# Fourier layer and soft mixture of experts on one core: the chains of batches 5 and 6 take the spacing of batches 0 to 4, and a product's scaling moves from VectorE to ScalarE and GpSimd

## The chip, the cores and the metric

The kernel runs on one core of a Trainium2 chip. The metric is device time in microseconds (us) of one launch. A core has five engines with a queue of instructions each: TensorE (PE in the rows; PEld is its weight load), VectorE (DVE), ScalarE (ACT), GpSimd (POOL) and SyncE (SP). Each executes its own instructions strictly in order, and waits on semaphores for the others. Nearly all DMAs are issued by SP's queue, also in order.

## The reference, cut to what matters

```python
X = rfft(x, axis=1)                         # x: 8 batches, 2496 rows, 256 columns
Yr = Xr @ w_r - Xi @ w_i + b_r
Yi = Xr @ w_i + Xi @ w_r + b_i
Y  = shrink(Yr, 0.01) + 1j * shrink(Yi, 0.01)
y  = irfft(Y, n=2496, axis=1)               # then all 8 * 2496 rows together:
logits = y @ phi                            # 32 slots, 4 for each of 8 experts
d  = softmax of logits over all rows
slot_input = d.T @ y
slot_out = for each expert: relu(slot_input[e] @ w1[e]) @ w2[e]
out = softmax(logits, over the 32 slots) @ slot_out
```

## The kernel before

**Transforms as products.** The length 2496 is 39 times 64. A first stage (products `pa`, results `ast`, written to DRAM as `adr`) transforms along 39. A second (`px`, read back as `ap`) transforms along 64. A batch then has five groups of four frequencies, and a group is one *step*: 40 steps in all, numbered s = 5 * batch + group. In a step PE computes `px` (two halves), `pk` and `py` (the linear layer), DVE and GpSimd form `rt` (the shrunk spectrum), and PE computes `pq` (the spectrum times phi, giving `p_sb`) and the transposes `pt`, whose copies `T` are kept until the batch's slots can be summed. To keep precision, fast products are made three times, from a value split into a rounded part (`xh`, `ch...`) and the rest (`xl`, `cl...`); the rounding is a copy, the rest a subtraction.

**The chain of a batch.** When its five steps are done, a batch b runs a chain beside the steps of the following batches (`c_stages`): the small spectrum `p_sb` is transformed back by `pg`, written to DRAM (`gd`), read back in another layout (`gp`), transformed by `pL` into logits `L`; `mx`, `pm`, `mall`, `pb` find and spread a running maximum; `ee` is the exponential; `pe` (to `ea`, DRAM `ed`, back as `eb`) and `pd` transform the exponentials forward; `dd` is `pd` times a constant, and the five products `pr` sum the slots out of `T` with `dd`. Batch 7, the last, has a chain of its own (`last_chain`), after which come the experts (`hps`, `po`) and the output.

**What sets the order.** Each piece of work is a generator that yields the time at which its next part is to be recorded, and a heap records them in that order; one unit of these times is a quarter of a step, a batch is 20 units. The times are hints for the order alone: they come from the table `PLAN`. In `c_stages` t0 is 20b + 26, and `pg`, `pL`, `pm`, `pb`, `pe`, `pd`, `pr` are offsets from it. `PLAN["late"]` replaces them for batches 4, 5 and 6. Before, batches 5 and 6 were packed closer than 0 to 4. TB (166) is the time at which the last step's own work ends.

**Places of tiles.** A tile is taken from one of a few pools under a tag with a fixed number of buffers, taken in turn; who takes one waits until its former content has been read. The transposes `pt` of batch 6 waited until after TB (`tp_t`, `late`), and its `rt` lay in buffers of the tag "T". `ps` is one bank of PSUM, used by `pg`, `pL`, `pm`, `pb`, `pe` and `pd` in turn.

**The product pd.** `halves` makes a product in two halves: it splits both sources (ACT rounds, `E_("cl_")`, DVE, subtracts), and for each half records the product and calls `evac`. For `pd` this was one DVE instruction that reads PSUM, multiplies by `dsc` and writes `dd`.

Of the kernel before, what the change touches and what calls it, by code (L numbers as in the profile page):

```python
# [23 lines left out]
S = 32  # L24
# [5 lines left out]
KG = 4  # L30
# [20 lines left out]
def _constants():  # L51
# [73 lines left out]
    "c0": 0.05,  # L125
    "pg": [1.35, 2.3],
    "pL": [6.6, 7.3],
    "pm": 8.35,
    "pb": 9.45,
    "pe": [11.35, 12.35],  # L130
    "cm": 14.3,
    "pd": [16.75, 17.5],
    "pr": [20.49, 24.49, 28.49, 32.489999999999995, 36.489999999999995],
    "au": [1.4, 18.85, 19.7],
    "tho": 1.4,
# [6 lines left out]
    "ko": 0.915,  # L142
    "to": 0.7,
    "ws": [-29, -28.9, -28.8, 2],
    "late": {'6': {'cms': [19.75, 19.71, 860.75, 862, 864, 865], 'pd': [20.36, 20.37], 'pr': [31.55, 31.6, 31.65, 31.7, 31.75], 'pL': [5.4, 5.8], 'pm': 6.875, 'pb': 7.325, 'pe': [8.75, 9.75], 'pg': [0.875, 1.275], 'fr': {'sinv': 0, 'm2': 0, 'f1': 0, 'suni': 0}}, '5': {'pg': [1.1, 1.8], 'pL': [4.95, 5.75], 'pm': 6.8, 'pb': 7.15, 'pe': [9.2, 9.9], 'pd': [13.8, 14.8], 'pr': [15.0, 17.25, 19.5, 21.75, 24.0]}, '4': {'pr': [18.4, 20.49, 24.49, 28.49, 32.49]}},
    "T_": {'wl': [[-45, 'r'], [-44, 'r'], [-43, 'r'], [-31.0, 't'], [-30.7, 't'], [-29.4, 't'], [-27.8, 't'], [-27.6, 't'], [-24, 't'], [-22, 't'], [-20, 't'], [-11, 'a'], [-10.3, 'a'], [-9.6, 'a'], [1.07, 'h'], [1.08, 'h'], [1.09, 'h'], [1.1, 'h'], [1.11, 'h'], [1.12, 'x'], [1.13, 'x'], [13.55, 'x'], [13.6, 'h'], [13.6, 'h'], [13.6, 'h'], [13.6, 'h'], [13.61, 't'], [13.61, 't'], [13.61, 't'], [13.61, 't'], [13.61, 't'], [13.7, 'T']], 'cl': 16, 'cp': 46.5, 'ct': 46.6, 'du': [[-4.5, 0], [-2.4, 0], [1.2, 0]], 'd1': [5, 2, 4, 0, 0, 0], 'cm': [19.9, 19.91, 19.92, 25, 25.1, 25.2], 'cm7': [18, 20, 22, 23, 25, 27], 'ye': 0.2, 'te': [[5.6, 0.2], [5.5, 0.4]], 'pg': [-7, -3.25, -0.35], 'yt': 0.5, 'wr': -30.6, 'tp': [0, 0.9, 1.05, 0.5], 'tt': [[-0.4, 0.5, 0.6, 0.7, 0.8], [12, 12.1, 12.2, 12.3, 12.4]], 'z': 13.55, 'th': [0.1, 0.12], 'tl': [0.2, 0.25]},
    "f1": [1.5, 2.15],
    "kw": [[-40, 9]],
# [35 lines left out]
def fourier_soft_moe_kernel(ctx: ExitStack, tc: tile.TileContext, t: dict, out: bass.AP):  # L184
# [207 lines left out]
    def f2(s, c, t0):  # L392
# [63 lines left out]
    def lin_y(s, e):  # L456
        b, grp = steps[s]
        end = s == ns - 1
        t0 = 4 * s + 1 + (PLAN["T_"]["ye"] if end else 1.35) * e
        yield t0  # L460
        py = psum("pl", f"py{b}_{grp}_{e}")
        lin(py, e, 0, xts[(s, 0)])
        if e == 1 and not end:
            t0 = 4 * s + 3
            yield t0
        lin(py, e, 1, xts[(s, 1)])
        t0 += 0.55 if e == 0 else PLAN["T_"]["yt"] if end else 0.3
# [156 lines left out]
    def c_stages(b):  # L624
# [74 lines left out]
        yield from halves(
            "suni", t0, K_["pd"], (f"pd{b}", lambda ps: ps[:, :320]), suni, fr,  # L700
            lambda h: eb[:, h * 10 : h * 10 + 10, :],
            lambda h, ps: V.tensor_tensor(
                out=dd[:, h * 10 : h * 10 + 10, :],
                in0=ps.rearrange("p (k s) -> p k s", s=S),
                in1=dsc[:, h * 10 : h * 10 + 10].unsqueeze(2).broadcast_to([128, 10, S]),
                op=ALU.mult,
            ),
        )
        yield t0 + K_["pd"][1] + 0.45
        zrow = wtile([1, 4, S], F32, "zrow", f"zrow{b}")  # L710
# [97 lines left out]
    ns = len(steps)  # L808
    TB = 4 * ns + LAG
    aps, xts, tts, psb, tls, kss = {}, {}, {}, {}, {}, {}  # L810
    step_to(setup())
    def one(tok):
        if tok[0] == "x":
# [446 lines left out]
```

## Time and profile before

| | |
|---|---|
| time, median of 3 runs | 574.54 us (573.51 to 575.91) |
| span of the profiled execution | 573.9 us |
| time of the profiled execution | not given apart; its span lies within the runs' range |
| PE busy | 530.5 us, 92% |
| DVE busy | 418.2 us, 73% |
| ACT busy | 299.4 us, 52% |
| POOL busy | 280.1 us, 49% |
| mean granted TensorE clock | 0.969 of full |

The span runs from the first to the last instruction. Until about 60 us the pipeline fills; from there to 383 us PE has the first stage of the next batch between its steps; from 383 to 461 us it has only the steps of batches 6 and 7 and the chains; then come batch 7's chain, and from about 496 us the experts and the output. A busy PE includes waits inside a pipelined product only in part, so waits are read from the views that name them.

### The profile page before, as it was taken

The numbers are of one execution on the slowest core, as the hardware profiler recorded it, in microseconds if no ns is written. First come the engines' busy times: TensorE is split into PE (matmuls) and PEld (weight loads), VectorE is DVE, ScalarE is ACT, GpSimd is POOL, SyncE is SP. The second block draws the span as 40 slices with busy tenths as digits, with TensorE's granted clock in tenths as the row PEclk, the third lists the DMA queues.
The fourth block names the chain that finished last, engine by engine and source line by source line (L and its number), as shares of the span: only waits on it lengthen the run. The fifth ranks groups of instructions, "written<-read, shape, count | busy, mean of one in ns | idle before, by whom it ended". The sixth has DMA issues, their size and how long they took to land.

```text
span 573.9 us, 11756 instructions
## 1 busy us (share of the span) xinstructions
PE 530.5 (92%) x4354; PEld 450.5 (78%) x4354; DVE 418.2 (73%) x837; ACT 299.4 (52%) x658; POOL 280.1 (49%) x258
## 2 busy tenths in 40 slices
PE   8679999999999999999999999988898988899894
PEld 4378999988898889889898889877786876467673
DVE  0346897699978997898899878958875663347783
ACT  4435555666566565666656566545323322137662
POOL 0046777766766586568565757663544310100100
PEclk9978999999999999999999999998899898999898
DMA  8888474766576747666757665945845257969898
GB/s 300 255 295 249 161 202 148 204 177 182 175 189 194 194 154 183 184 188 177 206 154 212 160 182 165 322 133 160 218 145 133 76 116 282 347 233 365 334 374 354
DMA packets 91760, 121.74 MB, mean 212 GB/s; under 512 B 46136, under 2 KB 67000, under 8 KB 91704
## 3 DMA queue, kind: packets, MB, share of 16 engines
q1 hardware_dynamic: 91448, 119.92, 67.7%
q10 hardware_dynamic: 256, 1.08, 0.5%
q8 instruction: 34, 0.56, 0.4%
q14 instruction: 22, 0.18, 0.1%
HBM read 69.98 MB, written 51.00 MB: 211 GB/s over the span
## 4 chain that ended last, share of the span: by engine, by line
PE 72%; DMA 10%; DVE 10%; ACT 3%; issue 2%; SPq 1%; ACTq 0%
PE py L243 16%; PE px L243 11%; PE pq L243 9%; PE pk L243 8%; PE pa L243 8%; PE pt L532 4%; PE pr L243 3%; DMA gp<-gd 3%; DMA gd<-g_sb 3%; PE pc L1064 2%; PE pL L243 2%; DMA ad<-ast 2%; DMA ap<-adr 2%; PE pe L243 1%; SPq L237 1%
## 5 line engine op out<-in xcount | busy, mean ns | idle before, releaser
L180 POOL TENSOR_TENSOR rt<-ut,rt 128x512 f32<-128x512 f32 x79 | 111.7, 1414 | 30.8 <-DVE rt L180 26.3
L180 POOL TENSOR_TENSOR xsl<-xsm,xsh 128x256 fp32r<-128x256 f32 x77 | 59.3, 770 | 108.9 <-DVE xsh L180 73.9
L180 POOL TENSOR_TENSOR xl<-xr,xh 117x512 fp32r<-117x512 f32 x73 | 97.7, 1338 | 23.0 <-ACT xh L180 15.0
L243 PE MATMUL px<-smov,ap 128*128 128x128 f32 x640 | 87.8, 282 | 7.2 <-DMA ap<-adr 2.7
L243 PEld LDWEIGHTS px<-smov,ap 128*128 128x128 f32 x640 | 82.3, 197 | 13.5 <-issue 7.7
L180 ACT CAST xth<-px 128x512 fp32r<-128x512 f32 x80 | 46.8, 585 | 76.9 <-PE px L243 38.5
L180 ACT COPY ast<-pa 128x512 f32<-128x512 f32 x86 | 50.3, 587 | 65.4 <-PE pa L243 63.5
L180 DVE SCALAR_TENSOR_TENSOR ut<-py,pk,k 128x256 f32<-128x256 f32 x160 | 69.5, 475 | 17.2 <-PE py L243 12.9
L180 DVE TENSOR_TENSOR xtl<-px,xth 128x512 fp32r<-128x512 f32 x80 | 54.6, 683 | 28.5 <-ACT xsm L180 22.8
L243 PE MATMUL py<-xth,nwsh 128*128 128x256 f32 x160 | 54.1, 338 | 0.0
L180 DVE TENSOR_SCALAR rt<-ut 128x512 f32<-128x512 f32 x69 | 52.2, 756 | 0.5
L243 PE MATMUL pk<-xsh,w_rh 128*128 128x256 f32 x160 | 49.5, 309 | 2.0 <-DVE xsh L180 2.0
L243 PE MATMUL pk<-xsl,w_rh 128*128 128x256 f32 x160 | 46.7, 292 | 0.0
L532 PE MATMUL pt<-pk,rt 128*128 128x128 f32 x320 | 45.9, 274 | 0.9 <-DVE dd L180 0.6
L180 ACT COPY T<-pt 128x512 f32<-128x512 f32 x70 | 41.9, 599 | 9.0 <-PE pt L532 7.1
L243 PE MATMUL pk<-xsh,w_rl 128*128 128x256 f32 x160 | 46.5, 290 | 0.0
L243 PE MATMUL py<-xth,nwsl 128*128 128x256 f32 x160 | 45.5, 284 | 0.0
L243 PE MATMUL py<-xth,wdl 128*128 128x256 f32 x160 | 45.3, 283 | 0.0
L243 PE MATMUL py<-xtl,nwsh 128*128 128x256 f32 x160 | 45.3, 283 | 0.0
L243 PE MATMUL py<-xth,wdh 128*128 128x256 f32 x160 | 45.1, 282 | 0.0
L243 PE MATMUL py<-xtl,wdh 128*128 128x256 f32 x160 | 45.1, 282 | 0.0
L243 PE MATMUL pq<-rhs,ct 128*128 128x512 f32 x156 | 43.2, 416 | 0.0
(187 smaller groups left out, 1251.2 us busy)
## 6 DMA issues: line engine op xcount, KB each, us to landing
ap<-adr SPq DMA_DIRECT2D x76, 256.0 KB
out<-ost SPq DMA_DIRECT2D x37, 512.0 KB
xr<-in_x SPq DMA_DIRECT2D x35, 512.0 KB
adr<-ast SPq DMA_DIRECT2D x20, 768.0 KB
w<-in_moe_w SPq DMA_DIRECT2D x28, 512.0 KB
adr<-ast SPq DMA_DIRECT2D x8, 512.0 KB
x<-in_x SPq DMA_DIRECT2D x11, 256.0 KB
ed<-ea SPq DMA_DIRECT2D x8, 330.0 KB
```

The costliest lines, as they stand in the source:

```text
L180: return lambda *a, **k: self.tc.keep_in_program_order(f(*a, **k))
L237: tc.keep_in_program_order(nc.sync.dma_start(**kw))
L243: tc.keep_in_program_order(nc.tensor.matmul(**kw))
L532: tc.keep_in_program_order(nc.tensor.transpose(out=out, in_=in_, identity=identity))
L1064: nc.tensor.transpose(out=pc[:, i * P1 : (i + 1) * P1], in_=chls[b][x][:, 2 * (r + i) : 2 * (r + i) + 2].rearrange("p g h s -> p (g h s)") ...
```

## The change

Batches 5 and 6 lose most of their own offsets. Batch 5 takes the common ones (`pL` at 6.6 and 7.3 where it had 4.95 and 5.75, `pe` 11.35 and 12.35 for 9.2 and 9.9, `pd` 16.75 and 17.75 for 13.8 and 14.8, `pr` 20.49 to 36.49 for 15 to 24). Batch 6 takes the common `pL`, `pm`, `pb`, `pe`; its `pg`, `pd`, `pr` stay. Batch 4 loses an earlier first `pr`. The common `pm` goes from 8.35 to 8.5. The first two groups of batch 6 (steps 30 and 31) put `rt` into the buffers of the earlier batches, and their transposes move into the main steps at times 134 and 138. Four loads `ap` (steps 33, 34, 38, 39) are recorded 1.5 to 2.5 units earlier. In the split of `pd`'s sources GpSimd takes DVE's subtraction. `pd`'s results are copied out of PSUM by ACT and then multiplied in place by GpSimd.

```diff
-    "pm": 8.35,
+    "pm": 8.5,
-    "pd": [16.75, 17.5],
+    "pd": [16.75, 17.75],
...
-    "cl_": 'V',
+    "cl_": {'sinv': 'VV', 'm2': 'VV', 'f1': 'VV', 'suni': 'PP'},
+    "pda": 1,
...
+    "apt": {34: 126.5, 33: 123.5, 39: 146.5, 38: 143.5},
+    "ne": 2,
+    "pdt": ('ps', 'ps'),
+    "t6": {30: 134, 31: 138},
...
+    def late_t(s):
+        return s >= ns - 10 + PLAN["ne"]
...
-        rt = wtile([128, KG, 2, 64], F32, "T" if b >= B - 2 else "rt", f"rt{b}_{grp}_{e}")
+        rt = wtile([128, KG, 2, 64], F32, "T" if late_t(s) else "rt", f"rt{b}_{grp}_{e}")
...
-            E_("cl_").tensor_tensor(out=xl, in0=x, in1=xh.bitcast(F32), op=ALU.subtract)
+            {"V": V, "P": P}[PLAN["cl_"][n][h]].tensor_tensor(out=xl, in0=x, in1=xh.bitcast(F32), op=ALU.subtract)
...
+        def scaled(h, ps):
+            hs = slice(h * 10, h * 10 + 10)
+            src, eng = ps.rearrange("p (k s) -> p k s", s=S), V
+            if K_["pda"]:
+                A.copy(out=dd[:, hs, :], in_=src)
+                src, eng = dd[:, hs, :], P
+            eng.tensor_tensor(
+                out=dd[:, hs, :], in0=src, in1=dsc[:, hs].unsqueeze(2).broadcast_to([128, 10, S]), op=ALU.mult
+            )
```

How this stands on the engines is shown at three places; names carry batch, group and half (`pL5_0` is the first half of batch 5's logits), and the number behind is a buffer's.

**PE, where batch 5's logits are made.** Before, directly behind the products `pq` of step 31 (batch 6, group 1):

```order
L243 MATMUL pr4_5287<-T4_2_1_4149,dd4_5066 32x256 x2
L243 MATMUL pq6_1_5537<-rt6_1_0_5346,pk0_112 32x128 x4
L243 MATMUL pq6_1_5537<-rt6_1_1_5415,pk0_112 32x128 x4
L243 MATMUL pL5_0_5548<-chpL5_0_5512,m2h_558 128x352
L243 MATMUL pL5_0_5548<-chpL5_0_5512,m2l_559 128x352
```

After the change, behind the twelve products `pk` of step 33:

```order
L248 MATMUL pk6_3_5578<-xsh6_3_1_5527,w_rl_229 128x256
L248 MATMUL pk6_3_5578<-xsl6_3_1_5528,w_rh_228 128x256
L248 MATMUL pL5_0_5599<-chpL5_0_5564,m2h_558 128x352
L248 MATMUL pL5_0_5599<-chpL5_0_5564,m2l_559 128x352
L248 MATMUL pL5_0_5599<-clpL5_0_5565,m2h_558 128x352
L248 MATMUL py6_3_0_5607<-xth6_3_0_5460,nwsh_234 128x256
```

Between the two places lie six products `py`, one transpose, a half of `px` and the twelve `pk`.

**GpSimd, beside batch 1's pd.** Before, in the steps 15 and 16 (batch 3):

```order
L180 TENSOR_TENSOR xl4_12_2641<-xr4_12_2477,xh4_12_2640 117x512
L180 TENSOR_TENSOR xsl3_1_1_2674<-xsm3_1_1_2672,xsh3_1_1_2673 128x256
L180 TENSOR_TENSOR rt3_0_0_2647<-ut3_0_0_2644,rt3_0_0_2647 128x512
L180 TENSOR_TENSOR xl4_14_2725<-xr4_12_2477,xh4_14_2724 117x512
L180 TENSOR_TENSOR rt3_0_1_2717<-ut3_0_1_2714,rt3_0_1_2717 128x512
```

After the change, at the same place:

```order
L185 TENSOR_TENSOR xl4_12_2643<-xr4_12_2479,xh4_12_2642 117x512
L185 TENSOR_TENSOR clpd1_0_2653<-eb1_2548,chpd1_0_2652 128x320
L185 TENSOR_TENSOR clpd1_1_2662<-eb1_2548,chpd1_1_2661 128x320
L185 TENSOR_TENSOR dd1_2551<-dd1_2551,pk1_113 128x320
L185 TENSOR_TENSOR xsl3_1_1_2676<-xsm3_1_1_2674,xsh3_1_1_2675 128x256
L185 TENSOR_TENSOR rt3_0_0_2649<-ut3_0_0_2646,rt3_0_0_2649 128x512
L185 TENSOR_TENSOR xl4_14_2728<-xr4_12_2479,xh4_14_2727 117x512
L185 TENSOR_TENSOR dd1_2551<-dd1_2551,pk1_113 128x320
```

Four instructions came in, three of them ahead of the `xsl` that the next `pk` needs.

**SP, where the steps end.** Before:

```order
L237 DMA ed6_6362<-ea6_6303 120x704
L237 DMA w13_6377<-in_moe_w1 128x1024
L237 DMA eb6_6379<-ed6_6362 64x20x32 x2
L237 DMA gd7_6437<-g_sb7_6436 64x12x32 x2
L237 DMA gd7_6437<-g_sb7_6436 64x4x32 x4
```

After the change:

```order
L242 DMA w13_6396<-in_moe_w1 128x1024
L242 DMA ed6_6459<-ea6_6380 120x704
L242 DMA gd7_6464<-g_sb7_6463 64x12x32 x2
L242 DMA eb6_6472<-ed6_6459 64x20x32 x2
L242 DMA gd7_6464<-g_sb7_6463 64x4x32 x4
```

The read `eb` of batch 6, which waits until the write `ed` has landed, now stands between the parts of batch 7's write `gd`.

## Rows read from the trace of the kernel before

**Rows 1.** Windows: stretch, busy us of PE, PEld, DVE, ACT, POOL, then PEclk, DMA.
```profile
100.00:350.00 250.00, 244.40 (x2166) 220.57 (x2166) 215.75 (x429) 154.86 (x344) 165.94 (x143) 1.00 0.65 184
388.00:393.00 5.00, 4.57 (x25) 4.48 (x26) 4.20 (x9) 2.86 (x8) 1.98 (x2) 0.67 0.49 148
410.00:419.00 9.00, 7.30 (x32) 6.64 (x33) 5.46 (x11) 3.10 (x8) 3.48 (x3) 0.62 1.04 311
444.00:450.00 6.00, 5.20 (x22) 4.14 (x23) 2.14 (x4) 2.17 (x6) 1.52 (x2) 0.72 0.55 182
```

**Rows 2.** PE's waits, 100 to 350 us: us in total, times, longest.
```profile
PE pm L659 <- DVE mx L180: 1.4, 4, 0.5
PE pd L243 <- ACT ast L180: 1.3, 2, 0.7
PE px L243 <- DVE xsm L180: 1.2, 2, 0.6
PE pd L243 <- DVE dd L180: 0.8, 2, 0.6
```

**Rows 3.** PE's waits, 350 to 466 us.
```profile
PE pL L243 <- ACT chpL L180: 3.1, 1, 3.1
PE pL L243 <- DMA gp<-gd: 2.1, 1, 2.1
PE pd L243 <- ACT chpd L180: 1.6, 1, 1.6
PE pd L243 <- DVE clpd L180: 0.8, 1, 0.8
```

**Rows 4.** Groups by shape, DVE and POOL, 100 to 350 us: busy, mean ns, idle before.
```profile
L180 DVE TENSOR_TENSOR clpd<-eb,chpd 128x320 fp32r<-128x320 f32 x8 | 6.4, 833 | 1.2 <-ACT chpd L180 1.1
...
L180 DVE TENSOR_TENSOR dd<-pd,pk 128x320 f32<-128x320 f32 x8 | 3.8, 480 | 0.0
...
L180 POOL TENSOR_TENSOR xl<-xr,xh 117x512 fp32r<-117x512 f32 x50 | 67.0, 1339 | 8.1 <-DVE xh L180 4.2 <-ACT xh L180 1.9 <-PE pa L243 0.8
...
L180 POOL TENSOR_TENSOR xsl<-xsm,xsh 128x256 fp32r<-128x256 f32 x46 | 36.1, 784 | 67.7 <-DVE xsh L180 40.9 <-PE pt L532 17.8 <-PE pa L243 4.8
```

**Rows 5.** Timeline of POOL beside batch 1's pd: start, us, instruction, idle before.
```profile
194.51 1.29 POOL L180 TENSOR_TENSOR xl<-xr,xh 117x512 fp32r<-117x512 f32 x1
200.31 0.72 POOL L180 TENSOR_TENSOR xsl<-xsm,xsh 128x256 fp32r<-128x256 f32 x1 [4.51 <-PE pt L532]
```

**Rows 6.** Timeline of ACT before batch 5's gd.
```profile
377.56 0.42 ACT L180 COPY g_sb<-pg 128x320 f32<-128x320 f32 x1
...
379.10 0.38 ACT L180 COPY xsm<-px 128x256 f32<-128x256 f32 x1
```

**Rows 7.** The chain of work that ended last, 384 to 476 us: start, us, what.
```profile
401.91 0.89 PE px L243 x8
402.80 1.41 PE pk L243 x12
...
407.24 0.57 PE pr L243 x8
407.81 0.48 PE pq L243 x16
...
456.24 0.69 PE pe L243 x2
...
458.46 2.84 PE py L243 x24
...
467.48 3.58 DMA gd<-g_sb
```

**Rows 8.** Timeline of SP's queue where the steps end.
```profile
460.55 1.38 SPq L237 DMA_DIRECT2D eb<-ed  x2
```

**Rows 9.** Timeline of PE, 461 to 477 us.
```profile
466.69 1.47 PE L532 MATMUL pt<-pk,rt 128*128 128x128 f32 x12
...
475.33 1.41 PE L243 MATMUL pL<-gp,pk 120*117 120x352 f32 x4 [3.65 <-DMA gp<-gd]
```

More of the change, by code (lines that the diff above doesn't have):

```diff
@@ L144 @@
     "ws": [-29, -28.9, -28.8, 2],
-    "late": {'6': {'cms': [19.75, 19.71, 860.75, 862, 864, 865], 'pd': [20.36, 20.37], 'pr': [31.55, 31.6, 31.65, 31.7, 31.75], 'pL': [5.4, 5.8], 'pm': 6.875, 'pb': 7.325, 'pe': [8.75, 9.75], 'pg': [0.875, 1.275], 'fr': {'sinv': 0, 'm2': 0, 'f1': 0, 'suni': 0}}, '5': {'pg': [1.1, 1.8], 'pL': [4.95, 5.75], 'pm': 6.8, 'pb': 7.15, 'pe': [9.2, 9.9], 'pd': [13.8, 14.8], 'pr': [15.0, 17.25, 19.5, 21.75, 24.0]}, '4': {'pr': [18.4, 20.49, 24.49, 28.49, 32.49]}},
+    "late": {'6': {'cms': [19.75, 19.71, 860.75, 862, 864, 865], 'pd': [20.36, 20.37], 'pdt': ('ps', 'pl'), 'pr': [31.55, 31.6, 31.65, 31.7, 31.75], 'pL': [6.6, 7.3], 'pm': 8.35, 'pb': 9.45, 'pe': [11.35, 12.35], 'pg': [0.875, 1.275], 'fr': {'sinv': 0, 'm2': 0, 'f1': 0, 'suni': 0}}, '5': {}, '4': {}},
     "T_": {'wl': [[-45, 'r'], [-44, 'r'], [-43, 'r'], [-31.0, 't'], [-30.7, 't'], [-29.4, 't'], [-27.8, 't'], [-27.6, 't'], [-24, 't'], [-22, 't'], [-20, 't'], [-11, 'a'], [-10.3, 'a'], [-9.6, 'a'], [1.07, 'h'], [1.08, 'h'], [1.09, 'h'], [1.1, 'h'], [1.11, 'h'], [1.12, 'x'], [1.13, 'x'], [13.55, 'x'], [13.6, 'h'], [13.6, 'h'], [13.6, 'h'], [13.6, 'h'], [13.61, 't'], [13.61, 't'], [13.61, 't'], [13.61, 't'], [13.61, 't'], [13.7, 'T']], 'cl': 16, 'cp': 46.5, 'ct': 46.6, 'du': [[-4.5, 0], [-2.4, 0], [1.2, 0]], 'd1': [5, 2, 4, 0, 0, 0], 'cm': [19.9, 19.91, 19.92, 25, 25.1, 25.2], 'cm7': [18, 20, 22, 23, 25, 27], 'ye': 0.2, 'te': [[5.6, 0.2], [5.5, 0.4]], 'pg': [-7, -3.25, -0.35], 'yt': 0.5, 'wr': -30.6, 'tp': [0, 0.9, 1.05, 0.5], 'tt': [[-0.4, 0.5, 0.6, 0.7, 0.8], [12, 12.1, 12.2, 12.3, 12.4]], 'z': 13.55, 'th': [0.1, 0.12], 'tl': [0.2, 0.25]},
@@ L165 @@
     "lsl": 'PPPPPPPPPPPPPPPPPPPPPPPV',
-    "ast4": {(0, 18): "wr", (1, 0): "wr", (1, 4): "ap"},
+    "ast4": {(0, 18): 'wr', (1, 0): 'wr', (1, 4): 'ap'},
+    "apt": {34: 126.5, 33: 123.5, 39: 146.5, 38: 143.5},
+    "ne": 2,
+    "pdt": ('ps', 'ps'),
+    "t6": {30: 134, 31: 138},
     "nd": 4,
@@ L535, in tp_t @@
         b, grp = steps[s]
-        late = b >= B - 2
-        n = TB + PLAN["T_"]["tt"][b - B + 2][grp] + 0.1 * h if late else 4 * s + LAG + PLAN["tt"][h]
+        late = late_t(s)
+        n = TB + PLAN["T_"]["tt"][b - B + 2][grp] + 0.1 * h if late else PLAN["t6"].get(s, 4 * s + LAG) + PLAN["tt"][h]
         yield n
-        if (grp, h) == (0, 0):
-            tls[b] = []
         pt = psum("pl" if late and h else "pt", f"pt{b}_{grp}_{h}")
@@ L550, in tp_t @@
             T = wtile([128, 2, D], F32, "T", f"T{b}_{grp}_{h}")
-        tls[b].append(T)
+        tls[b][2 * grp + h] = T
         copy((A, V)[h] if late else E_("te"), T.rearrange("p k d -> p (k d)"), pt)
@@ L579, in c_comb, with halves @@
             cins[b] = [cb[:P1, :GX, :], cb[:P1, GX:, :]]
-    def halves(n, t0, times, out, const, fr, src, evac):
+    def halves(n, t0, times, out, const, fr, src, evac, tags=("ps", "ps")):
         xs = []
@@ L596, in halves @@
             yield t0 + times[h]
-            ps = psum("pl" if n == "suni" and h and not fr[n] else "ps", f"{out[0]}_{h}")
+            ps = psum(tags[h], f"{out[0]}_{h}")
             if fr[n]:
@@ L701, in c_stages @@
             lambda h: eb[:, h * 10 : h * 10 + 10, :],
[L702 to L707, printed above, removed]
+            scaled,
+            K_["pdt"],
         )
@@ L810, in fourier_soft_moe_kernel @@
     aps, xts, tts, psb, tls, kss = {}, {}, {}, {}, {}, {}
+    tls.update({b: [None] * (2 * NGRP) for b in range(B)})
     step_to(setup())
@@ L895, in ap_load @@
     def ap_load(s):
-        yield 4 * s - 7
+        yield PLAN["apt"].get(s, 4 * s - 7)
         aps[s] = load_ap(*steps[s])
```

## The prediction

> **What bounds the kernel now.** I read the windows first, then PE's waits, then the rows around each wait. From 100 to 350 us PE is busy for 244.4 of 250 us at the full clock, DVE for 215.8, GpSimd for 165.9 [rows 1]: PE is the bound there, DVE comes next, and only what makes PE wait can be won. The waits that carry names come to 4.7 us [rows 2]. The reader is to see that the chains of the batches cause them: `pm` waits for `mx`, `pd` for the bank `ps`, which `dd` empties (where ACT is named, ACT had other work, and `dd` stood in DVE's queue), and `px` for a DVE that is behind.
>
> After 350 us the picture changes. Four waits of 0.8 to 3.1 us, 7.6 us together, stand before `pL` and `pd` of batches 5 and 6 [rows 3], and behind each PE runs slowly: the granted clock is 0.67 from 388 to 393 us, 0.62 from 410 to 419, 0.72 from 444 to 450, a mixture of 2.4 and 1.2 GHz, with PE busy 4.57, 7.30 and 5.20 us [rows 1]. So a wait there costs its own length and then up to (1 - 0.67) x 4.57 + (1 - 0.62) x 7.30 + (1 - 0.72) x 5.20 = 1.5 + 2.8 + 1.5 = 5.8 us more. Together the stalls of the late stage cost 13.4 us. It is the largest thing in this profile that an order can win.
>
> **The spacing of batches 5 and 6, -13.4 us and +1.0.** For `pL` of batch 5 PE arrives later by the work that now stands ahead of it: six `py` (a quarter of 2.84, 0.71), a half of `px` 0.89, twelve `pk` 1.41 [rows 7], a transpose of about 0.1 (a quarter of a `pt` group, [rows 9]), so 3.1 us, as long as the wait was. But its source moves too. The second `g_sb` copy now stands behind ACT's two copies of the `px` half: it would start where `xsm` ends, at 379.5 instead of 377.56 [rows 6], less about 0.7 us because that `px` no longer has half a `pg` ahead of it (taken like half a `pe`, 0.69 [rows 7]). So `gd`, and with it `gp`, start 1.2 us later, and a wait of up to 1.2 us stays. The two `ap` reads that were issued behind `gp` now go ahead of `gd`, so `gp` should fly a little faster: I take 0.8, between 0 and 1.2.
>
> For `pd` of batch 5 the work between the second `pe` and `pd` grows by a `pr` 0.57, a `pq` 0.48, two groups of `pt` at 1.47 / 3 = 0.49 and a transpose [rows 7, 9]: 2.1 us against a wait of 2.4 [rows 3]. About 0.2 stays. GpSimd may be inside an instruction of 1.3 us [rows 4] when its subtraction for `pd` is due, so up to 1.5 can stay. For `pL` of batch 6, PE arrives 0.89 + 1.41 + 0.1 = 2.4 us later, and the wait was 2.1: gone. Sum of what stays: 1.0, between 0 and 3. If the waits shrink to this, the slow stretches go too; I count them whole.
>
> **The main stage, -3.3 us.** `pm` now stands behind `pq`, which is 0.48 us of work [rows 7] against waits of at most 0.5 [rows 2]: 1.4 won. ACT's copy of 128x320 out of PSUM takes 0.42 us [rows 6], and ACT is busy for 155 of 250 us [rows 1], so `ps` is free before `pd`'s second half comes, and the 2.1 us of `pd` waits go. GpSimd's price for 128x320 is not in the trace; from 784 ns for 256 columns and 1339 for 512 [rows 4] a straight line gives 0.92 us, four a batch 3.7 us. Its subtractions start when the `xl` ahead ends (195.8), the first is done at 196.7, close to where `pd`'s third product wants it: I charge 0.2 us a batch, 0.8 in four. DVE loses two subtractions of 833 ns and two products of 480 [rows 4], 2.6 us a batch; half of the `px` waits, 0.6, should go with them. 1.4 + 2.1 - 0.8 + 0.6 = 3.3, between 0 (GpSimd late each time) and 4.7 (all).
>
> What hides GpSimd's 3.7 us is its own gap: beside batch 1's `pd` it stands idle 4.5 us before the next `xsl` [rows 5], and that gap is waiting for DVE. Queued behind the new `dd` product, which waits for ACT and PE, is the `xsl` that `pk` needs; DVE should hand over its source about 2 us earlier, so `xsl` has room. Without this cover each added instruction would cost its 0.92 us.
>
> On that very place a page speaks against the change. DVE's subtraction with both sources in SBUF takes 833 ns on average, its product of the same size out of PSUM 480 [rows 4]. The Trainium skill, SBUF — State Buffer, "Who interferes with whom", says that a DVE instruction with two SBUF inputs and a GpSimd instruction that reads SBUF lock each other out for a whole instruction; Perfetto Trace Analysis, "Optimizing Scalar/DVE Operations", adds that moving work between the two therefore might not help. The trace fits such a lock. By the rule the main stage would win nothing; the second rival below is what that gives here.
>
> **The transposes of batch 6 and the end of the steps, +2.3 us.** Four groups of `pt`, 4 x 0.49 = 2.0 us, leave a place where PE then waits 3.65 us for `gp` of batch 7 anyway [rows 9], and enter the steps. What counts at the end is SP's queue. Before, `eb` of batch 6 was issued at 460.55, 3.6 us after its second `pe` ended at 456.93 [rows 7, 8], ahead of `gd` of batch 7. Now both halves of `pe` follow the last `py`. In the clock of before, that `py` ended at 461.3 [rows 7]; two `pe` (1.4) and two `pr` (1.1) leave the front, the transposes (2.0) enter it: 460.8. Then `pe`, `pq`, `pe`, 1.9 us: 462.7, and 3.6 later, at 466.3, `eb` can be issued. It takes 1.38 on SP, to 467.7, and only then come the four last `gd`, at 0.69 each: the last starts at 469.7 instead of 467.48 [rows 7]. The chain of batch 7 hangs on it: +2.2 us. `pd` of batch 6, in PE's order ahead of the remaining `pt`, will wait for `eb` until about 471, with PE idle; the `pt` behind it should be through before `gp` lands near 477.5: 0.1, and up to 3 if PE's clock is down by then. In all +2.3, between 0 and 5.
>
> The moved `ap` reads, batch 4's later `pr` and the buffers of `rt` cost nothing: a buffer of "T" that batch 7 takes is freed by a `pr` one step ahead, about 9 us; if that cover were gone, DVE's `rt` and then `pq` would wait.
>
> **Sum.** 573.9 - 13.4 + 1.0 - 3.3 + 2.3 = 560.5 us, against the span of the profiled execution, 0.6 below the median of 574.54; I make no correction for that.
>
> **The rivals.**
> - *The late waits move along.* In-order queues keep batch 5's and 6's data late: ACT waits for `gp` ahead of its `px` copies, SP for `ed`. For it: DVE was busy 4.2 of 5 us from 388 to 393 [rows 1], so the late steps have little room. Against it: batches 0 to 3 use these offsets with no `pL` wait in rows 2, though their steps are longer. Half of the 13.4 stays: 560.5 + 6.7 = 567.2.
> - *The lock between DVE and GpSimd eats the main gain.* Six batches give GpSimd 3.7 us each and take 2.6 from DVE; if DVE is shut out throughout, 1.1 x 6 = 6.6 us are added and the 3.3 not won: 570.4. Against it: GpSimd's gap of 4.5 us [rows 5].
> - *Slower: GpSimd comes onto the path to `pk`.* If in six batches `xsl` is late by all four added instructions, 3.7 x 6 = 22.2 us are added and the 3.3 not won: 586. It is slower than before by the bound below from (573.9 + 2.9 - 563.8) / 6 = 2.2 us a batch on. For it: the new instructions stand ahead of `xsl`, and one waits for PE itself. Against it: GpSimd idles 84 of 250 us.
> - *More is won than counted:* no new wait, nothing lost at the end: 573.9 - 13.4 - 4.7 = 555.8, and less where a restart costs more than its row.
>
> **How the numbers follow.** Chances: the forecast 0.60 (its own range 557 to 565), more won 0.10, waits move along 0.18, the lock 0.06, slower 0.06. The range 552 to 569 leaves out the last two and a part of the third, under 2 in 10. A change of 0.5%, 2.9 us, is about what a measurement of this kernel can tell from none. The forecast, more won and waits that move along are faster by more, and half of the lock: 0.90; the other half is within, with part of the slower rival's lower end: 0.05; slower 0.05.
>
> **What would show it.** PE's waits on `pL` and `pd` between 350 and 450 us together under 2 us and the clock 1.00 there; from 100 to 350 us no `pm` wait, `pd` waits under 1 us, `xsl` not late. GpSimd's `clpd` and `dd` at 0.8 to 1.0 us; DVE about 15 us less busy. At the end a PE idle stretch of about 5 us before batch 6's `pd`, released by `eb`. It would be wrong if a `pk` waits for `xsl`, if `gp` still ends waits of 2 us or more, or if the first `pL` of batch 7 comes over 5 us later behind the last `py` than before (14 us).

## The result and the profile after

The changed kernel takes 554.36 us (median of 4 runs, 552.34 to 557.89), the kernel before beside it 575.22 (573.51 to 577.14). The ratio is 0.965, its 95% interval 0.9587 to 0.9713. The profiled execution took 552.34 us, with a span of 550.5.

The page of the changed kernel gives busy time by engine, and the granted clock in 40 slices:

```profile
PE 520.6 (95%) x4354; PEld 444.9 (81%) x4354; DVE 407.4 (74%) x809; ACT 304.8 (55%) x674; POOL 302.4 (55%) x284
...
PEclk9889999999999999999999999999999989999898
```

Between the two profiled executions the span differs by 23.4 us, between the medians the time by 20.9: the profiled execution of after is the fastest of its four, and that of before ran at a mean granted clock of 0.969, where other executions of the same kernel had 0.960 to 0.985.

To see where the 23.4 us of span went, the starts of the same products are laid side by side, taken from the timelines of PE. The first `pk` of batch 1 is the beginning of the main stage, the first `pk` of batch 6 its end, and the last `py` ends the steps.

| | before | after | difference |
|---|---|---|---|
| first pk of batch 1 | 83.69 | 81.84 | -1.85 |
| first pk of batch 6 | 356.55 | 348.43 | -8.12 |
| end of the last py | 461.30 | 437.47 | -23.83 |
| first pL of batch 7 | 475.33 | 453.09 | -22.24 |
| end of the span | 573.9 | 550.5 | -23.4 |

So the main stage gave 8.12 - 1.85 = 6.3 us, the late steps 15.7, the end of the steps took 1.6 back, and the tail gave 1.2. The first 1.85 lie ahead of the first changed instruction; the other kernels of this study, equal up to there, come there 0.1 to 2.5 us earlier than before, so that much is difference between executions. Of the tail's 1.2, 0.9 lies in batch 7's chain from `pL` to `pe`, which took 6.24 us before (475.33 to 481.57) and 5.34 after (453.09 to 458.43).

The windows cut at these points, of before:

```profile
83.70:356.60 272.90, 267.30 (x2383) 241.48 (x2381) 233.11 (x464) 168.78 (x373) 183.08 (x159) 1.00 0.64 181
356.60:461.30 104.70, 95.99 (x825) 83.25 (x828) 75.96 (x161) 42.21 (x99) 52.39 (x51) 0.93 0.59 171
```

and of after, with the stretch behind the last `py`:

```profile
81.80:348.40 266.60, 265.60 (x2381) 241.52 (x2380) 225.19 (x447) 170.78 (x381) 196.95 (x175) 1.00 0.66 185
348.40:437.30 88.90, 86.98 (x818) 79.10 (x817) 74.78 (x152) 44.88 (x105) 59.35 (x59) 1.00 0.71 198
437.50:453.10 15.60, 12.00 (x88) 8.23 (x86) 6.25 (x12) 4.70 (x13) 2.54 (x3) 0.89 0.54 116
```

In the main stage PE's idle time fell from 5.6 to 1.0 us. In the late steps it fell from 8.7 to 1.9, and the granted clock rose from 0.93 to 1.00: PE was busy 9.0 us less for the same products.

PE's waits of after, 100 to 350 us, answer to [rows 2]:

```profile
PE pt L540 <- DVE p_sb L185: 0.5, 2, 0.2
PE pd L248 <- POOL clpd L185: 0.2, 1, 0.2
PE pL L248 <- DVE clpL L185: 0.2, 1, 0.2
```

The waits on `pm`, `px` and, but for 0.2 us, `pd` are gone. From 350 to 436 us, against [rows 3], the longest that are left are

```profile
PE pm L665 <- DVE mx L185: 0.8, 1, 0.8
PE pL L248 <- DMA gp<-gd: 0.5, 1, 0.5
```

The groups of GpSimd's two new instructions (100 to 350 us, busy and mean ns), against the estimates from [rows 4]:

```profile
L185 POOL TENSOR_TENSOR clpd<-eb,chpd 128x320 fp32r<-128x320 f32 x8 | 7.4, 949 | 0.0
L185 POOL TENSOR_TENSOR dd<-dd,pk 128x320 f32<-128x320 f32 x8 | 6.0, 749 | 0.4 <-ACT dd L185 0.4
```

Where the steps end, SP's queue of after, against [rows 8]:

```profile
439.97 0.34 SPq L242 DMA_DIRECT2D ed<-ea  x1
441.41 1.28 SPq L242 DMA_DIRECT2D gd<-g_sb  x2
442.82 1.42 SPq L242 DMA_DIRECT2D eb<-ed  x2
444.33 2.92 SPq L242 DMA_DIRECT2D gd<-g_sb  x4
448.66 1.05 SPq L242 DMA_DIRECT2D gp<-gd  x3
```

and PE of after, against [rows 9]:

```profile
443.19 0.71 PE L248 MATMUL pg<-p_sb,pk 128*128 128x128 f32 x4
447.36 1.41 PE L248 MATMUL pd<-eb,pk 128*128 128x320 f32 x2 [3.46 <-DMA eb<-ed]
...
450.48 2.48 PE L540 MATMUL pt<-pk,rt 128*128 128x128 f32 x20
453.09 1.41 PE L248 MATMUL pL<-gp,pk 120*117 120x352 f32 x4
```

PE no longer stands idle before `pL`: the transposes end at 452.96, and by the chain of work that ended last `gp` lands at 452.95. The idle time stands before batch 6's `pd`. That chain runs in the profile of after over `ed`, SP, `gd` and `gp`:

```profile
439.97 2.79 DMA ed<-ea
446.64 1.97 DMA gd<-g_sb
449.39 3.56 DMA gp<-gd
```

and before, behind the `gd` of [rows 7]:

```profile
471.84 3.36 DMA gp<-gd
```

### The profile page after: what moved, and what is told of

Its sections match the earlier page's. It is cut to its first block, busy times and chain, and to the rows that moved or that the text cites. A ratio compares the mean times of both kernels' runs of the same rounds, so it can differ in the third digit from the quotient of the medians.

```text
span 550.5 us, 11772 instructions
## 1 busy us (share of the span) xinstructions
PE 520.6 (95%) x4354; PEld 444.9 (81%) x4354; DVE 407.4 (74%) x809; ACT 304.8 (55%) x674; POOL 302.4 (55%) x284
## 4 chain that ended last, share of the span: by engine, by line
PE 78%; DVE 8%; DMA 6%; issue 3%; ACT 2%; SPq 1%; POOL 1%; ACTq 0%; POOLq 0%; DVEq 0%
PE py L248 18%; PE px L248 11%; PE pa L248 10%; PE pq L248 9%; PE pk L248 8%; PE pt L540 5%; PE pr L248 3%; DMA gp<-gd 2%; PE pc L1078 2%; DMA gd<-g_sb 2%; PE pL L248 2%; PE pe L248 2%; SPq L242 1%; PE pd L248 1%; PE hps L248 1%
## 5 line engine op out<-in xcount | busy, mean ns | idle before, releaser
L248 PE MATMUL px<-smov,ap 128*128 128x128 f32 x640 | 86.0, 279 | 3.9 <-DMA pk<-in_pk 2.4
L185 DVE SCALAR_TENSOR_TENSOR ut<-py,pk,k 128x256 f32<-128x256 f32 x160 | 69.5, 475 | 18.6 <-PE py L248 15.3
L248 PE MATMUL pk<-xsh,w_rh 128*128 128x256 f32 x160 | 47.8, 299 | 1.3 <-DVE xsh L185 1.3
L185 ACT COPY T<-pt 128x512 f32<-128x512 f32 x72 | 43.2, 601 | 4.7 <-PE pt L540 4.4
L248 PE MATMUL pk<-xsl,w_rh 128*128 128x256 f32 x160 | 45.5, 285 | 0.0
L248 PE MATMUL pk<-xsh,w_rl 128*128 128x256 f32 x160 | 45.1, 282 | 0.0
```

What stands on the lines that cost most here:

```text
L185: return lambda *a, **k: self.tc.keep_in_program_order(f(*a, **k))
L248: tc.keep_in_program_order(nc.tensor.matmul(**kw))
```

## The experiments

The theory was that of the prediction: the spacing removes the late stalls and the slow clock behind them, the moved work frees `pd` and `px` in the main stage, and the end of the steps gives some back. The rivals were waits that move along, the lock between VectorE and GpSimd, and GpSimd on the path to `pk`. Each kernel was timed in five rounds beside the kernel before, whose median was 571.3 to 575.2 us from one set of rounds to the next; so kernels are compared by their ratios.

**One half of the change alone.** Spacing, with both pieces of moved work taken out:

```diff
-    "cl_": {'sinv': 'VV', 'm2': 'VV', 'f1': 'VV', 'suni': 'PP'},
-    "pda": 1,
+    "cl_": {'sinv': 'VV', 'm2': 'VV', 'f1': 'VV', 'suni': 'VV'},
+    "pda": 0,
```

> The changed kernel with VectorE doing the subtraction and the scaling of pd again: only the spacing, the transposes' place and pm's place are left of the change. Theory A (two gains that add up: the spacing wins about 15 us after 350 us, the work taken from VectorE about 5 us before it): 559 to 561 us, 0.974 of before; between step 5's pk and step 30's pk the time is as long as before less the 1.4 us of the pm waits, and the waits of 0.4 to 0.8 us before pd are back. Rival B (the gain before 350 us comes from pm's place and from nothing else): 554 to 556, no difference from the changed kernel. Rival C (the late stage needed VectorE's relief as well, since it was busy 9 tenths there): 564 or more, with waits for VectorE on pL and pd of batch 5 of 1 us and more.

Measured: 559.46 us, ratio 0.9721 (0.9681 to 0.9761), as theory A had it.

The moved work alone, with the kernel before's offsets, reads `ap` and transposes; PE's and SP's order is that of before:

```diff
+    "cl_": {'sinv': 'VV', 'm2': 'VV', 'f1': 'VV', 'suni': 'PP'},
+    "pda": 1,
```

> The kernel before with only the split and scaling of pd moved to ScalarE and GpSimd; the orders of PE and SP are those of before. Theory A: 569 to 571 us, 0.99 of before; no wait of pd for dd, no px wait for VectorE from 100 to 350 us; the waits before pL and pd of batches 5 and 6 stay at 7 us. Rival B: 574 to 576, no difference. The rule on the lock between VectorE and GpSimd: 574 to 580, VectorE's rt and casts longer by as much as was taken away. Rival C: 565 or less.

Measured: 566.13 us, ratio 0.9852 (0.9809 to 0.9895). It gains 8 us where 4 were expected, between theory A and rival C: no time is lost on balance to a lock, and the forecast's price of this half is too small. In ratio the two halves give 2.8% and 1.5%, 4.3% together, against 3.5 (2.9 to 4.1) for both at once. The profiles show where they overlap. On the main stage, the late steps and the stretch from the last `py` to `pL` of batch 7, the moved work alone takes 4.8, 3.2 and 2.4 us off the kernel before; beside the new spacing it takes off 4.3, 0.9 and -0.1 (the spacing alone against the changed kernel). The 2.4 lie in two transfers, `gd` 1.98 us instead of 3.58 and `gp` 2.58 instead of 3.36, and no run ties them to the moved work.

**Parts of the moved work.** With the new spacing, the split on GpSimd alone, and the scaling by ScalarE and GpSimd alone:

```diff
-    "pda": 1,
+    "pda": 0,
```

> The changed kernel with the split of pd's sources on GpSimd alone; pd's result is again multiplied out of PSUM by VectorE in one instruction. The neighbours are the run with neither (559.5) and the changed kernel with both (554.4). Theory A (VectorE was late for px and had a queue ahead of dd; each of the two edits takes work from it, so each wins a part): px waits gone or under 0.4 us, pd waits half of the 2.3 us of the run with neither, 556.5 to 558. Rival B (the two engines lock each other out, the subtraction on GpSimd only moves the time): 559 to 561 and px waits of 1 us as with neither. Rival C (all is won by VectorE's relief, whichever edit brings it): 554 to 556.

```diff
-    "cl_": {'sinv': 'VV', 'm2': 'VV', 'f1': 'VV', 'suni': 'PP'},
+    "cl_": {'sinv': 'VV', 'm2': 'VV', 'f1': 'VV', 'suni': 'VV'},
```

> The changed kernel with the copy by ScalarE and the product by GpSimd alone; the split of pd's sources is on VectorE again. Theory A (the bank ps is emptied early by ScalarE, VectorE is relieved by 2 times 0.48 us a batch): the pd waits named dd or ast are gone, px waits of 0.5 to 1.1 us stay, 555.5 to 557.5. Rival B (lock; the whole gain is from this edit): 554 to 555. Rival C (the gain is that of the split): 558.5 to 560.5.

Measured: the split alone 553.0 us, ratio 0.9665 (0.9613 to 0.9717); the scaling alone 558.1, 0.9748 (0.9698 to 0.9799). The main stage in the profiles (the first `pk` of batch 1 to that of batch 6, and PE's busy time in the windows of 100 to 350 us):

| | main stage against before | PE busy, 100 to 350 us |
|---|---|---|
| neither | -2.0 | 245.75 |
| scaling alone | -2.9 | 246.93 |
| split alone | -5.5 | 248.24 |
| both | -6.3 | 249.00 |

The split brings nearly all of it, though it leaves `dd` on VectorE: rival C of the first holds for it, but not in its "whichever edit", since the scaling alone cannot be told in time from neither (0.9721). PE's waits of the split alone, 100 to 350 us, show neither `px` nor `dd`:

```profile
PE pt L540 <- DVE p_sb L185: 1.3, 4, 0.4
PE pd L248 <- POOL clpd L185: 0.2, 1, 0.2
```

and the scaling alone, which removes these waits too, has one on GpSimd instead:

```profile
PE pa L248 <- POOL xl L185: 1.4, 3, 0.5
```

GpSimd's queue stands idle there for 6.8 us before its eight `dd`, until ScalarE's copy comes; in the changed kernel it is 0.4:

```profile
L185 POOL TENSOR_TENSOR dd<-dd,pk 128x320 f32<-128x320 f32 x8 | 6.0, 749 | 6.8 <-ACT dd L185 6.8
```

So `pd` did not need another engine to empty the bank: it was enough that VectorE came to `dd` earlier, without the subtractions ahead of it in its queue.

**More work on GpSimd at the same place.** Behind each `dd` two, then four, further subtractions of a value from itself, into a buffer that nothing reads any more:

```diff
             evac(h, out[1](ps))
+            if n == "suni" and fr[n]:
+                for _ in range(2):
+                    P.tensor_tensor(out=xs[h][1], in0=xs[h][0].bitcast(F32), in1=xs[h][0].bitcast(F32), op=ALU.subtract)
```

> The changed kernel with more work on GpSimd at the place of the change: behind each product dd two further subtractions of 128x320 (of a value from itself, into a buffer that nothing reads any more), so four more a batch at 0.86 to 1.08 us, as clpd takes in the profile of the changed kernel: 3.5 to 4.3 us a batch on top of 3.4. Theory A (GpSimd's gaps ahead of xsl, 4 us at the longest and 42 us together from 100 to 350 us, take it up): 554 to 557, PE's waits for POOL under 2 us. Rival B (xsl and with it pk is late by all of what is added, as in the slower rival of the prediction): four to six times 3.5 to 4.3, so 568 to 580. Rival C (VectorE and GpSimd lock each other out, VectorE pays a part): instructions of VectorE with two sources in SBUF longer than before, and waits of PE for DVE; 557 to 568.

> The same with four further subtractions behind each dd, so eight more a batch, 7 to 8.6 us on top of 3.4. Theory A (the gaps take up what fits: 4 us of gap stand behind the two places where 3.5 to 4.3 us each are put, and what is over makes pk wait for xsl, or pa for xl): PE waits for POOL of 2 to 10 us in all, 556 to 566. Rival B (all of it on the path): 582 to 606. Rival C (lock): as A or longer, with longer instructions of VectorE and PE waiting for DVE above all.

Measured: 561.55 us, ratio 0.9796 (0.9759 to 0.9834), and 582.44 us, 1.0163 (1.012 to 1.0206). The added instructions took 776 and 818 ns on average, so with 24 and 48 of them 18.6 and 39 us were added. Against the changed kernel's 0.965 that cost 1.5% and 5.1%, 8.4 and 29 us: nearly half of the first dose and three quarters of the second. PE's waits of the first (60 to 500 us):

```profile
PE pa L248 <- POOL xl L185: 1.6, 5, 0.4
PE pk L248 <- POOL xsl L185: 1.4, 1, 1.4
```

and of the second:

```profile
PE pk L248 <- POOL xsl L185: 10.9, 6, 2.9
PE pq L248 <- POOL rt L185: 9.3, 5, 1.9
```

Theory A fell for both: the gaps do not take up even the first dose. The second comes out at the lower end of rival B; PE waits for GpSimd 20.7 us there with the smaller waits, some 3.4 for each of six batches, above the 2.2 from which the prediction had this rival decide, and the kernel is slower than before. The first lies in rival C's range, but the waits that grew are for GpSimd, not for VectorE; they come to 3.4 of the 8.4 us, and no row names the rest. The lock is there all the same. VectorE's own subtraction of 128x320 with both sources in SBUF, in the groups of 100 to 350 us (mean ns behind the busy time), before the change, after it, with the first dose, with the second, and with the split alone:

```profile
L180 DVE TENSOR_TENSOR clpg<-p_sb,chpg 128x320 fp32r<-128x320 f32 x9 | 5.0, 556 | 0.0
```

```profile
L185 DVE TENSOR_TENSOR clpg<-p_sb,chpg 128x320 fp32r<-128x320 f32 x8 | 5.4, 672 | 0.0
```

```profile
L185 DVE TENSOR_TENSOR clpg<-p_sb,chpg 128x320 fp32r<-128x320 f32 x9 | 8.6, 959 | 0.0
```

```profile
L185 DVE TENSOR_TENSOR clpg<-p_sb,chpg 128x320 fp32r<-128x320 f32 x9 | 7.6, 844 | 0.0
```

```profile
L185 DVE TENSOR_TENSOR clpg<-p_sb,chpg 128x320 fp32r<-128x320 f32 x9 | 4.9, 544 | 0.0
```

The mean does not follow GpSimd's load: it falls from the first dose to the second, and the split alone, which adds to GpSimd's work, has the shortest. What counts is whether GpSimd is inside an instruction when VectorE's begins. The first `clpd` of batch 1, in the trace of before, begins 1.03 us before GpSimd's `xl` of [rows 5] ends (195.80), and ends 0.34 us behind it:

```profile
194.77 1.37 DVE L180 TENSOR_TENSOR clpd<-eb,chpd 128x320 fp32r<-128x320 f32 x1 [0.31 <-ACT chpd L180]
```

The fourteen profiles have 216 of these subtractions (`clpg`, and `clpd` where VectorE makes it). The 91 that found GpSimd idle took 476 to 493 ns; the 114 that began with over 0.12 us of a GpSimd instruction still to run ended 0.34 to 0.35 us behind the end of that instruction. VectorE's subtraction `xtl`, of which one source is in PSUM, does not wait: its 73 took 671 to 693 ns in the trace of before, though 28 of them began beside a running GpSimd instruction. Its mean stays the same, before and with the first dose:

```profile
L180 DVE TENSOR_TENSOR xtl<-px,xth 128x512 fp32r<-128x512 f32 x46 | 31.3, 681 | 11.2 <-ACT xsm L180 11.2
```

```profile
L185 DVE TENSOR_TENSOR xtl<-px,xth 128x512 fp32r<-128x512 f32 x46 | 31.3, 679 | 6.2 <-ACT xsm L185 6.0
```

**The four reads ap.** The prediction had put them at nothing. Put back to their old place in the changed kernel:

```diff
-    "apt": {34: 126.5, 33: 123.5, 39: 146.5, 38: 143.5},
+    "apt": {},
```

> The changed kernel, with the four reads ap of steps 33, 34, 38 and 39 recorded where they were before, so that they stand behind gp of the chains in SP's queue. Theory A (the earlier reads let gp of batch 5 and 6 fly faster, and are otherwise free): waits of PE on pL for gp grow from 0.5 us to 0.5 to 1.7 us, the time is 554.4 to 556. Rival B (an ap read that is issued late makes px late): a wait of PE's px for ap of over 0.5 us appears, 555 to 558. Rival C (their place is of no account): the same waits within 0.3 us, 554 to 555.

Measured: 559.09 us, ratio 0.9781 (0.9732 to 0.9829), 1.3% or 7 us more than with them moved; in the profiles the late steps take 96.5 us instead of 89.0. Rival B holds, beyond its own range. SP's queue of this kernel, the reads for step 39 behind `gp` of batch 6, which waits for `gd`:

```profile
415.55 1.38 SPq L242 DMA_DIRECT2D gd<-g_sb  x2
420.65 1.05 SPq L242 DMA_DIRECT2D gp<-gd  x3
421.80 1.26 SPq L242 DMA_DIRECT2D ap<-adr  x2
```

and what PE then does:

```profile
427.04 2.05 PE L248 MATMUL px<-smov,ap 128*128 128x128 f32 x8 [4.51 <-DMA ap<-adr]
```

Behind it the granted clock is 0.77 from 427 to 440 us, and the eight products of `px` take 2.05 us instead of 1.05 in the same view of the changed kernel (421.81). In the changed kernel these reads leave at 408.51, ahead of that `gd`:

```profile
408.51 1.24 SPq L242 DMA_DIRECT2D ap<-adr  x2
415.00 1.42 SPq L242 DMA_DIRECT2D gd<-g_sb  x2
```

Then the reads alone, in the kernel before:

```diff
+    "apt": {34: 126.5, 33: 123.5, 39: 146.5, 38: 143.5},
-        yield 4 * s - 7
+        yield PLAN["apt"].get(s, 4 * s - 7)
```

> The kernel before, with nothing changed but the four reads ap of steps 33, 34, 38 and 39, which are recorded 1.5 to 2.5 units earlier; only SP's queue differs. Put back behind gp in the changed kernel they cost 5 to 6 us, because px of step 39 then waited 4.5 us for ap. Theory A (in the old spacing PE comes to that px late, behind its own wait for gp, and the read lands in time anyway: the reads alone win nothing, they only have to go along with the new spacing): ratio 0.997 to 1.003, and no px wait for ap in either. Rival B (the early reads also free gp of batches 5 and 6 and shorten their flight, as the prediction took for 0 to 1.2 us): PE's wait of 2.1 us on pL for gp shrinks by 0.5 us or more, ratio 0.99 to 0.997.

Measured: 570.51 us, ratio 0.9966 (0.9928 to 1.0004), on the border of A and B, and the time does not tell them apart. The profile speaks for B: the wait for `gp` of batch 6 shrank from 2.1 [rows 3] to 0.7 us and that before `pL` of batch 5 from 3.1 to 2.1, while `pd` of batch 5 waited 2.3 us as before (2.4), and the late steps took 101.8 us instead of 104.8. What the reads are worth hangs on the spacing: without it up to 3 us in one profile, which the time cannot tell from no change; with it 7 us.

**The common pm at its old offset:**

```diff
-    "pm": 8.5,
+    "pm": 8.35,
```

> The changed kernel with pm at 8.35 instead of 8.5, which moves it ahead of pr and pq again in batches 0 to 4; nothing else differs on any engine. Theory A with the waits of the profile: pm waits of 0.3 to 0.5 us are back in five batches, 1.4 to 2.5 us: 556 us, at the edge of what is measured. Rival B (pm's place is the whole gain before 350 us): 559 to 560. Rival F (with VectorE relieved mx is ready in time anyway): 554, no difference.

Measured: 555.09 us, ratio 0.9666 (0.9627 to 0.9706). The time cannot tell it from the changed kernel; the trace shows the `pm` waits back, 2.0 us in four from 100 to 350 us, and a main stage 2.2 us longer, which is A's mechanism.

**The end of the steps.** Batch 6's `pL`, `pm`, `pb`, `pe` at their old offsets:

```diff
-'pL': [6.6, 7.3], 'pm': 8.35, 'pb': 9.45, 'pe': [11.35, 12.35]
+'pL': [5.4, 5.8], 'pm': 6.875, 'pb': 7.325, 'pe': [8.75, 9.75]
```

> The changed kernel with batch 6's pL, pm, pb and pe at their old offsets (5.4, 5.8, 6.875, 7.325, 8.75, 9.75). Theory A: batch 6's pL waits for gp again, 2 to 3 us and 1.5 us of slow clock, but pe and ed come earlier, so that eb is no longer between the parts of batch 7's gd: 4.5 lost and up to 2.2 won, 556 to 557 us, 0.968. Rival D (what the close spacing of batch 6 won at the end is worth more than its wait): 552 to 553. Rival E (batch 6 carries most of the late gain): 560 and more.

Measured: 556.94 us, ratio 0.9694 (0.9645 to 0.9743). The last `py` ends 2.6 us later than in the changed kernel, but the first `pL` of batch 7 starts 13.3 us behind it instead of 15.6 and only 0.3 later in all: what batch 6's new offsets win in the steps is nearly all given back at their end. The time lies where theory A had it, but its interval does not part it from the changed kernel's.

Two attempts to keep both. One moves `pe` of batch 6 ahead and its `pd` behind the transposes, the other issues half of batch 7's `gd` by ScalarE's queue, with the same `pd`:

```diff
-'pd': [20.36, 20.37],
+'pd': [20.91, 20.92],
-'pe': [11.35, 12.35]
+'pe': [11.06, 11.08]
```

> The changed kernel, with the first pe of batch 6 between the two halves of the last py and the second right behind them, and pd of batch 6 behind all transposes pt instead of around the first. Theory A (at the end of the steps PE stands idle 3.5 us before pd for eb, and the transposes queued behind it then delay the first pL of batch 7): ed and eb leave about 1 us earlier, the transposes run in that idle time, and the first pL of batch 7 starts 14.2 to 15 us behind the end of the last py instead of 15.6; 553 to 554. Rival B (gp of batch 7 lands only then anyway, since gd stands behind eb): PE waits for gp instead, pL 15.4 to 16 us behind, 554 to 555. Rival C (pe waits for ee, and the last py with it): 555 to 556.

```diff
-'pd': [20.36, 20.37],
+'pd': [20.91, 20.92],
...
-            sp(out=gd[c, k0:k1].rearrange("k n s -> n k s"), in_=g_sb[c * N2 : c * N2 + N2, k0:k1, :])
+            (aq if c and k1 - k0 < K1 else sp)(out=gd[c, k0:k1].rearrange("k n s -> n k s"), in_=g_sb[c * N2 : c * N2 + N2, k0:k1, :])
```

> The changed kernel, with half of batch 7's six writes gd issued by ScalarE's queue instead of SP's, and pd of batch 6 behind all its transposes pt. Theory A (behind the last g_sb SP's queue sets when gp of batch 7 can go: four gd at 0.73 us, two of which now go beside the others; PE has its transposes done in the idle time before pd): gp leaves SP 1 to 1.6 us earlier against the last py than in the changed kernel (11.35 us behind it there), the first pL of batch 7 starts 13 to 14.6 us behind the last py instead of 15.8; ratio 0.960 to 0.964. Rival B (the writes themselves, not their issue, set when gp goes): gp leaves under 0.5 us earlier, ratio 0.964 to 0.966. Rival C (ScalarE's copies behind the issues are late): pL 16 us or more behind the last py.

Measured: 553.96 us, ratio 0.9683 (0.9633 to 0.9733), and 554.0 us, 0.9667 (0.9621 to 0.9713). Neither beats the changed kernel; the rivals B hold. (The second expectation counts from 437.31, where `pe` begins, and so has 15.8 for the 15.6.) The first `pL` of batch 7 starts 15.5 us behind the last `py` in both, and PE now waits for `gp`, in the second for 4.12 us:

```profile
447.06 1.32 PE L248 MATMUL pd<-eb,pk 128*128 128x320 f32 x4 [0.25 <-DMA eb<-ed]
452.49 2.67 PE L248 MATMUL pL<-gp,pk 120*117 120x352 f32 x4 [4.12 <-DMA gp<-gd]
```

There the last `gd` had left SP at 445.7 and `gp` at 447.80, 2.1 us behind; in the changed kernel it was 447.25 and 448.66, 1.4 behind. Against the last `py` the issue ends 1.1 us earlier and `gp` starts 0.4 earlier: most of what is won in issuing is lost again while the write lands. That the second queue is the reason is not shown: in the profile of before, with one queue, `gp` followed the last `gd` by 3.0 us (468.10 and 471.10). And the chain that follows ran slower. The window from `pL` to `pe` of batch 7, in this kernel and in the changed one:

```profile
452.40:460.00 7.60, 7.40 (x30) 5.75 (x30) 3.18 (x10) 1.80 (x5) 0.00 (x0) 0.63 1.02 394
```

```profile
453.00:458.50 5.50, 4.79 (x30) 3.81 (x30) 3.86 (x11) 1.82 (x6) 0.00 (x0) 1.00 1.01 397
```

Behind the wait of 4.12 us the granted clock is 0.63, and the chain to `pe` takes 7.4 us; behind the transposes, without a wait, it is 1.00, and 5.3. The other profiles agree: behind 4.96 us (the first of the two attempts) 0.67 and 7.4, behind 4.70 (batch 6's old offsets) 0.70 and 7.1, behind 3.65 (before) 0.73 and 6.2, behind 2.05 (the moved work alone) 1.00 and 5.35.

## Why the prediction was right, and which terms were off

The time lies in the range, but below the forecast's own 557 to 565, in the rival "more won than counted", which had a chance of 0.10; the mechanism was right in its large term and the sizes of the terms were off. The span of 550.5 lies 10.0 us below the 560.5: 2.8 from the late steps, 3.0 from the main stage, 1.2 from the end of the steps, and 1.2 and 1.85 from the tail and the beginning, for which the sum had no term. All of them erred to the same side, and the 1.85 are luck.

**The late stalls, -13.4 + 1.0.** With -0.5 for the work that changes places ahead of the last `py`, 12.9 us were forecast up to its end; 15.7 were measured. Idle time fell by 6.8 us, which is 7.6 - 1.0 to 0.2 us. The mis-sized term is the slow clock: 5.8 us from three windows, while busy time fell by 9.0. The granted clock over the whole stretch would have said (1 - 0.93) x 95.99 = 6.7; of the rest, 0.5 is the moved work and 1.8 is not named by a row. The spacing alone brings 14.8 of it (19.2 - 4.4 at the same two points). How much of the 9.0 belongs to the one execution of before stays open: the moved work alone keeps the old spacing and idles 8.1 us in its late steps, yet has 93.5 us busy at a clock of 0.97. Against its 101.5 us the changed kernel's 89.0 are 12.5 less, close to the 12.9. Of the new waits, neither the 0.8 for `pL` of batch 5 nor the 0.2 for its `pd` came; the 0.5 us for `gp` stand before `pL` of batch 6 (at 424.74), where the prediction had none, and the 0.8 before batch 6's `pm` were not foreseen. The rival that the waits move along is refuted.

**The main stage, -3.3.** Measured -6.3, of which 4.6 us are idle time. The terms: `pm` 1.4 as forecast, though its view has a fifth wait that [rows 2] leave out, 0.5 us on ScalarE's `xth`, which went too (the spacing alone, where up to there little but `pm` and the second half of `pd` has another offset, has 245.75 - 244.40 = 1.4 us less idle time). The moved work was put at 2.1 - 0.8 + 0.6 = 1.9 and gave 249.00 - 245.75 = 3.2 us of idle time: all of the `px` waits went and not half, and GpSimd was late once, by 0.2 us, and not four times. The prediction also put its price on the wrong half: ScalarE's copy does take away the 2.1 us of `pd` waits, as forecast, but the split alone takes them away as well, and only the split shortens the stage by more than 1 us. The other 1.7 us are less busy time for the same products (267.30 to 265.60); a busy PE holds part of the waits inside a product, and no row says which.

**The transposes and the end, +2.3.** With the 0.5 counted above, 2.8 were forecast from the last `py` on; measured 15.6 - 14.0 = +1.6. The place and the path were right: the chain shown above runs from `pe` over `ed` and `eb` in SP's queue to the last `gd`, which begins its flight 9.2 us behind the last `py` instead of 6.2, 3.0 later where 2.7 were forecast (8.9). The mis-sized term is the flight, which the sum took as unchanged: `gd` took 1.97 us instead of 3.58 [rows 7], `gp` 3.56 instead of 3.36. Why `gd` was faster no run shows. But `eb` was not alone in it. ACT's timeline of after has the two copies that the last four `gd` need:

```profile
443.71 0.49 ACT L185 COPY g_sb<-pg 128x128 f32<-128x128 f32 x2 [2.32 <-PE pg L248]
```

They end at 444.20, the first of them at 443.98, and `eb` had left SP at 444.24, so it held the `gd` up by 0.4 us at most. Just as late is `pg`: it starts at 439.96, 2.5 us behind the last `py`, where it was 0.5 before (461.81), since both `pe` and a `pr` now stand ahead of it. With the first `pe` moved ahead, `pg` started 1.5 us behind the last `py`, but all six `gd` stood behind `eb`, and the last began its flight 10.1 us behind instead of 9.2. With batch 6's old offsets both come earlier, and `pL` 13.3 us behind the last `py`.

**What was put at nothing.** Moving the `ap` reads cost nothing, but the prediction did not see that the spacing needs them: PE no longer waits for `gp`, so it reaches the next `px` before a read that stands behind `gp` has landed. Without them 7 of the 20 us are lost. For the buffers of "T" and batch 4's `pr` no wait of PE appeared.

**The rivals on GpSimd.** The lock is real and was weighed rightly. The rule of the Trainium skill, SBUF — State Buffer, "Who interferes with whom", agrees with this case's traces (476 to 493 ns beside an idle GpSimd, up to 1.57 us beside a running one, against 671 to 693 with a source in PSUM). The caution of the Trainium skill, Perfetto Trace Analysis, "Optimizing Scalar/DVE Operations", that such a move might not help, did not hold here: the moved work won 1.5% by itself. VectorE's subtraction took 833 ns on average [rows 4], and 476 at the least in that trace, since four of those eight waited for GpSimd, and stood ahead of what PE needed next; on GpSimd it takes 949 ns and fits. VectorE pays some of it back: it is 10.8 us less busy, not 15. The gap of 4.5 us in [rows 5], taken for a wait on VectorE, ended by its row with PE's `pt`, 0.1 us behind VectorE's `xsh`. How near GpSimd is to the path was underrated: of four more instructions a batch, half their time shows.

**The signs.** Clock 1.00 up to the last `py`, no `pm` wait up to 350 us, `clpd` at 949 ns, an idle PE before batch 6's `pd` (3.46 us for about 5) and `pL` of batch 7 1.6 us later came as told; `dd` at 749 ns is a little below.

## What to carry to other kernels

Before a wait is moved, look at what stands behind it in the in-order queue that it also holds, and move that too: here four reads that cost at most 3 us where they stood cost 7 us once PE came earlier. When two engines lock each other, ask which of them stands nearest to the bound one, and not which is faster: a subtraction that took longer on GpSimd than on VectorE still took 3.5 us out of the main stage. An idle time behind which the engine has work to do before the next wait can be better than a wait right ahead of the critical product, because the clock is back by then: in the changed kernel it is 0.71 from `pd` to `pL` (447.36 to 453.09) and 1.00 behind.

## What was not expected of the hardware

The same subtraction of 128x320 on VectorE took from 476 ns to 1.37 us in the trace of before, and what decided it was how long GpSimd's instruction of that moment still had to run: VectorE's ended 0.34 to 0.35 us behind it. With two queues the six writes `gd` were issued 1.1 us earlier, and the read behind them started only 0.4 earlier; the flight of the last `gd` was 1.97 to 3.58 us from one profile to another, for no reason that a run shows. And behind a wait of about 4 us the granted clock was 0.63 in the 7.6 us that followed, where it stayed at 1.00 without a wait: `pL` came 15.5 us behind the last `py` instead of 15.6, but the tail took 100.0 us instead of 97.4.
